# Two heads beside each other in PSUM: 64-column matmuls in the first batch's query phase

## The chip, the cores and the metric

The kernel runs on one core of a Trainium2 chip. The core has five engines that work side by side, each on its own list of instructions in a fixed order: PE (matrix multiply, whose weight loads the profile lists apart as PEld), DVE (elementwise work and reductions), ACT (activation functions and copies), POOL (elementwise work, SBUF only) and SP, which here starts most of the DMA transfers. SBUF is the working memory of 128 partitions. PSUM is the memory that PE writes its sums to; here it is used as tiles of 128 partitions by 512 floats. The metric is the time of one execution in microseconds (us).

## The reference, cut to what matters

```python
# q, k, v: (8 batches, 8 heads, 576 tokens, 64); w_phi: (64, 128)
def phi(x):
    proj = einsum('bhsd,df->bhsf', x, w_phi)
    proj = proj - max(abs(proj), axis=-1, keepdims=True)
    return concatenate([exp(proj), exp(-proj)], axis=-1)     # 256 features
q_p, k_p = phi(q), phi(k)
kv  = einsum('bhsf,bhsd->bhfd', k_p, v)
z   = sum(k_p, axis=2)
num = einsum('bhsf,bhfd->bhsd', q_p, kv)
den = einsum('bhsf,bhf->bhs', q_p, z)[..., None] + 1e-6
x   = (num / den), tokens by heads*64                        # 4608 x 512
h   = x @ w_in                                               # 512 -> 2048
out = maximum(0.01 * h, h) @ w_out                           # 2048 -> 512
```

It is linear attention with an exponential feature map, followed by a two-layer network over all 4608 tokens. All of it is float32.

## The kernel before, in words

Two heads make a pair: partitions 0 to 63 hold the first, 64 to 127 the second. A batch has four pairs. Attention of a pair has a key phase, which sums `kv` and `z` over the tokens, and a query phase, which gives `num` and `den` for each token and divides. The network runs over blocks of 256 tokens; its matmuls split float32 into a high and a low part (`xh`, `xl`, `w0h`, `w0l`, `gh`, `gl`) and are most of PE's work. A tile program schedules all instructions: the code gives priorities (`tc.cur_priority`), the scheduler weighs them with estimated times and so fixes each engine's order when the kernel is built. A change of a few instructions can therefore move others anywhere in the program.

The first batch is special. Its four key phases (`first_k_phase`) run at the very start. Its query phase (`first_q_phase`) runs by token units instead of pair by pair: unit 0 is tokens 0 to 255, unit 1 tokens 256 to 511 (four pairs each, one group of instructions per pair), unit 2 the last 64 tokens of all four pairs in one group. That makes nine groups. After unit 0 the first block of the network can begin, after unit 1 the second. Meanwhile `load_weights` (lines 187 to 197) prepares the network's weights, three ACT, DVE and POOL steps for each of 32 slices.

One group of the query phase goes like this. PE projects the tokens (L440). DVE takes the largest absolute value and subtracts it (L523, L525). PE transposes the result (L531) into PSUM. ACT computes both exponentials for both heads, `ee[0]` and `ee[1]` (L538, L539); the tiles are `eq` or `qs` in the profile. PE then multiplies by the pair's `kvs_of` (tiles `f`), whose 128 columns are the 64 columns of `kv` and 64 copies of `z`: for one head, partitions 0 to 63 of the PSUM tile `nm` receive the numerator and 64 to 127 the denominator (L553). The two heads `j` stand beside each other along the free dimension. ACT copies each head's numerator into the ring of attention outputs (L556, tile `ring`) and its denominator, with 1e-6 added, into `dn` (L557), each on 64 partitions. DVE transposes `dn`, takes the reciprocal of one value per token and transposes back (L560, L562, L563, tile `mb`), and POOL multiplies (`x`, L74). `nm` is tile `h` in unit 0 (two buffers) and tile `c` in units 1 and 2 (one buffer). The tile `dn` has two buffers.

A float32 matmul of this phase is one instruction in the program and two records in the profile, each with its own weight load. The network's split matmuls (L611 to L633, type fp32r) make one.

Of the kernel before, what the change touches and what calls it, by code (L numbers as in the profile page):

```python
# [13 lines left out]
AF = mybir.ActivationFunctionType  # L14
# [31 lines left out]
def attention_moe_kernel(ctx: ExitStack, tc: tile.TileContext, q, k, v, w_phi, w_in, w_out, out):  # L46
    nc = tc.nc
# [8 lines left out]
    def st(shape, dt, tag, name=None):  # L56
        return pools.get(tag, sp).tile(shape, dt, tag=tag, name=name or tag, bufs=BUFS.get(tag, 1))
# [18 lines left out]
    def pt(tag):  # L76
        return ps.tile([P, 512], F32, tag=tag, name=tag, bufs=PBUFS[tag])
# [140 lines left out]
    kvs_of = {}  # L218
# [290 lines left out]
    def first_q_phase(u):  # L509
        t0, w = units[u]  # L510
        rq = first_q[u]
        tail = u == 2
        if tail:
            rq = rq.rearrange("p a t -> p (a t)").unsqueeze(1)
            w = NP * w
        n, ns = P, 2
        for hp in range(1 if tail else NP):
# [14 lines left out]
            if hp % 2:  # L532
                ee = st([P, 2, S], F32, "qs")
                ee = [ee[:, t, 0 : 2 * w] for t in range(2)]
            else:
                ee = [st([P, 2, U], F32, "eq").rearrange("p a b -> p (a b)")[:, 0 : 2 * w] for t in range(2)]
            ee = [x.rearrange("p (j t) -> p j t", j=2) for x in ee]
            nc.scalar.activation(ee[0], tr, AF.Exp)  # L538
            nc.scalar.activation(ee[1], tr, AF.Exp, scale=-1.0)  # L539
            yield  # L540
            nm = pt("c" if u else "h")[:, 0 : 2 * w].rearrange("p (j t) -> p j t", j=2)
            dn = st([P, U], F32, "dn")[:, 0:w]
            x = ring[:, 0, :, t0:S] if tail else ring[:, 0, hp : hp + 1, t0 : t0 + w]
            m = x.shape[1]

            def heads(y):
                return y.rearrange("p (a t) -> p a t", a=m)

            for j in range(2):
                for h in range(m):  # L550
                    ts = slice(w // m * h, w // m * h + w // m)
                    for t in range(2):
                        nc.tensor.matmul(nm[:, j, ts], lhsT=kvs_of[hp + h][0][:, j, t], rhs=ee[t][:, j, ts],  # L553
                                         start=t == 0, stop=t == 1)
                rr = slice(64 * j, 64 * j + 64)
                nc.scalar.copy(x[rr], heads(nm[0:64, j]))  # L556
                nc.scalar.activation(dn[rr], nm[64:128, j], AF.Copy, bias=1e-6)  # L557
            yield
            dt = st([P, U], F32, "mb")[:, 0:w]
            nc.vector.transpose(dt, dn)  # L560
# [96 lines left out]
    together(first_k_phase(0), first_k_phase(1))  # L657
    together(first_k_phase(2), first_k_phase(3))
    together(first_q_phase(0))
    split(0)  # L660
    tc.cur_priority = PU
    first_load_q(1)
    first_load_q(2)
    together(first_q_phase(1))
    split(1, *xb)
    together(first_q_phase(2))
    for t in range(TT):
        accs[1, t] = pt(('h', 'a')[t])
# [59 lines left out]
```

## Time and profile before

| what | value |
|---|---|
| three runs, median (lowest to highest) | 1168.24 us (1168.23 to 1170.24) |
| the profiled execution's own time | 1168.86 us |
| its span in the profile | 1167.1 us |
| PE busy over the span | 1141.4 us (98%) |
| DVE, ACT, POOL busy | 737.9, 854.7, 652.0 us |
| the matmuls of L553 start between | 40.1 and 83.5 us |
| ACT in L556 and L557, 18 instructions each | 6.54 and 6.85 us |

The span is what the profiler saw from the first to the last instruction; the time of an execution has 1.8 us more around it. In rows of the profile a line such as `L553 PE MATMUL c<-eq,f 128*128 128x64 f32 x32` names the line of the kernel, the engine, the operation, the tile written and the tiles read, the part of the PE array used (rows*columns), the shape and the number of records. A row of waits names the waiting engine and line, what it waited for, the total in us, how often, and the longest. Rows of the chain give start, length and the work that held up the end.

### The profile page before, as it was taken

The numbers are of one execution on the slowest core, as the hardware profiler recorded it, in microseconds if no ns is written. First come the engines' busy times: TensorE is split into PE (matmuls) and PEld (weight loads), VectorE is DVE, ScalarE is ACT, GpSimd is POOL, SyncE is SP. The second block draws the span as 40 slices with busy tenths as digits, with TensorE's granted clock in tenths as the row PEclk, the third lists the DMA queues.
The fourth block names the chain that finished last, engine by engine and source line by source line (L and its number), as shares of the span: only waits on it lengthen the run. The fifth ranks groups of instructions, "written<-read, shape, count | busy, mean of one in ns | idle before, by whom it ended". The sixth has DMA issues, their size and how long they took to land.

```text
span 1167.1 us, 21441 instructions
## 1 busy us (share of the span) xinstructions
PE 1141.4 (98%) x7496; PEld 1024.0 (88%) x7496; DVE 737.9 (63%) x1316; ACT 854.7 (73%) x2256; POOL 652.0 (56%) x702
## 2 busy tenths in 40 slices
PE   8899999999999999999999999999999999999998
PEld 5677778899999999889999999999899999999997
DVE  6878996587767767767777767646777675100000
ACT  5777786888887888878888888868888885433232
POOL 1451222567666677676777666766566665433232
PEclk9999999999999999999999999999999999999999
DMA  8435432211111111101111111101111100000000
GB/s 222 139 90 153 123 102 53 60 43 33 52 34 51 34 41 34 51 23 34 49 25 52 33 52 34 52 12 41 34 51 34 41 2 12 10 20 10 10 19 19
DMA packets 69980, 57.87 MB, mean 50 GB/s; under 512 B 52208, under 2 KB 53488, under 8 KB 69872
## 3 DMA queue, kind: packets, MB, share of 16 engines
q1 hardware_dynamic: 67120, 55.78, 17.0%
q8 instruction: 59, 0.97, 0.3%
q10 hardware_dynamic: 2752, 0.72, 0.3%
q14 instruction: 49, 0.40, 0.1%
HBM read 46.27 MB, written 9.44 MB: 48 GB/s over the span
## 4 chain that ended last, share of the span: by engine, by line
PE 80%; DVE 8%; ACT 5%; DMA 3%; issue 2%; POOL 1%; SPq 1%; ACTq 0%; DVEq 0%; POOLq 0%
PE h L611 10%; PE h L612 10%; PE h L614 10%; PE acc L631 10%; PE acc L632 10%; PE acc L633 10%; PE c L242 7%; PE a L419 3%; PE a L424 2%; PE a L421 2%; PE a L265 2%; DVE tq L396 1%; PE a L379 1%; PE a L380 1%; PE h L476 1%
## 5 line engine op out<-in xcount | busy, mean ns | idle before, releaser
L74 POOL TENSOR_TENSOR gl<-g,gh 128x256 fp32r<-128x256 f32 x288 | 236.7, 825 | 311.7 <-ACT gh L69 226.9
L611 PE MATMUL h<-xh,w0h 128*128 128x256 f32 x1088 | 275.5, 282 | 3.3 <-ACT g L618 1.6
L612 PE MATMUL h<-xh,w0l 128*128 128x256 f32 x1088 | 272.7, 280 | 0.0
L611 PEld LDWEIGHTS h<-xh,w0h 128*128 128x128 f32 x1088 | 205.1, 189 | 14.0 <-ACT g L618 3.1
L631 PE MATMUL acc<-w1h,gh 128*128 128x512 f32 x544 | 214.3, 394 | 0.1
L632 PE MATMUL acc<-w1l,gh 128*128 128x512 f32 x544 | 213.4, 392 | 0.0
L612 PEld LDWEIGHTS h<-xh,w0l 128*128 128x128 f32 x1088 | 205.0, 188 | 7.7
L633 PE MATMUL acc<-w1h,gl 128*128 128x512 f32 x544 | 204.6, 394 | 0.3 <-POOL gl L74 0.3
L614 PE MATMUL h<-xl,w0h 128*128 128x256 f32 x1088 | 191.7, 281 | 0.0
L618 ACT ACTIVATE g<-h 128x256 f32<-128x256 f32 x288 | 108.5, 380 | 100.8 <-PE h L614 81.7
L74 POOL TENSOR_TENSOR ql<-eq,qh 128x576 fp32r<-128x576 f32 x96 | 145.4, 1527 | 45.2 <-DVE qh L410 39.9
L69 ACT CAST gh<-g 128x256 fp32r<-128x256 f32 x288 | 115.1, 402 | 62.3 <-PE acc L632 60.7
L614 PEld LDWEIGHTS h<-xl,w0h 128*128 128x128 f32 x1088 | 155.6, 189 | 0.8 <-issue 0.4
L74 POOL TENSOR_TENSOR kpl<-ek,kph 128x512 fp32r<-128x512 f32 x72 | 103.1, 1432 | 75.7 <-ACT kph L69 58.9
L71 DVE COPY o<-acc 128x512 f32<-128x512 f32 x17 | 11.7, 688 | 165.2 <-DMA out_dram<-o 125.1
L633 PEld LDWEIGHTS acc<-w1h,gl 128*128 128x128 f32 x544 | 100.1, 188 | 15.9 <-POOL gl L74 1.0
L631 PEld LDWEIGHTS acc<-w1h,gh 128*128 128x128 f32 x544 | 102.3, 188 | 12.2 <-ACT kvl L192 0.4
L632 PEld LDWEIGHTS acc<-w1l,gh 128*128 128x128 f32 x544 | 102.3, 188 | 11.3
L295 ACT ACTIVATE ek<-pmk,m4n 128x128 f32<-128x128 f32 (+1 forms) x240 | 90.1, 392 | 10.4 <-DVE m4n L279 7.7
L296 ACT ACTIVATE ek<-pmk,m 128x128 f32<-128x128 f32 (+1 forms) x240 | 89.4, 390 | 10.3 <-DVE m L273 8.5
L410 DVE TENSOR_REDUCE qh<-eq 128x576 fp32r<-128x576 f32 x96 | 69.6, 751 | 26.3 <-ACT eq L404 23.6
L270 DVE TENSOR_TENSOR pmk<-a,pmk 128x256 f32<-128x256 f32 (+1 forms) x120 | 49.2, 419 | 51.9 <-ACT pmk L69 50.3
(186 smaller groups left out, 2382.4 us busy)
## 6 DMA issues: line engine op xcount, KB each, us to landing
out_dram<-o SPq DMA_DIRECT2D x36, 256.0 KB, 2.0
rv<-in_v_dram SPq DMA_DIRECT2D x28, 320.0 KB, 3.6
rq<-in_q_dram SPq DMA_DIRECT2D x28, 288.0 KB, 2.9
rk<-in_k_dram SPq DMA_DIRECT2D x27, 288.0 KB, 2.9
ring<-in_w_in_dram SPq DMA_DIRECT2D x9, 512.0 KB, 3.6
f<-in_w_out_dram SPq DMA_DIRECT2D x7, 512.0 KB, 3.7
f<-in_w_in_dram SPq DMA_DIRECT2D x7, 512.0 KB, 3.7
ring<-in_w_out_dram SPq DMA_DIRECT2D x5, 512.0 KB, 6.0
```

The costliest lines, as they stand in the source:

```text
L69: nc.scalar.copy(o, i)
L74: (nc.vector if pick(key) == "v" else nc.gpsimd).tensor_tensor(o, a, b, op=op)
L242: nc.tensor.matmul(kvp[0 : lt.shape[1], 256 * j : 256 * j + 256], lhsT=lt, rhs=rt, start=first and j == 0, stop=last, skip_group_check=True)
L295: nc.scalar.activation(ek[r, j, 0:F], pmk[r, h], AF.Exp, bias=m4n[r, h : h + 1])
L296: nc.scalar.activation(ek[r, j, F:256], pmk[r, h], AF.Exp, scale=-1.0, bias=m4[r, h : h + 1])
L611: nc.tensor.matmul(ph, lhsT=weight(0, "h", ft)[:, d * P : d * P + P], rhs=xh[d], start=d == 0, stop=False)
L612: nc.tensor.matmul(ph, lhsT=weight(0, "l", ft)[:, d * P : d * P + P], rhs=xh[d], start=False, stop=False)
L614: nc.tensor.matmul(ph, lhsT=weight(0, "h", ft)[:, d * P : d * P + P], rhs=xl[d], start=False, stop=d == NP - 1)
L618: nc.scalar.activation(g, ph, AF.Prelu, alpha=0.01)
L631: nc.tensor.matmul(a, lhsT=gh[:, ts], rhs=weight(1, "h", ft), start=ft == 0, stop=False)
L632: nc.tensor.matmul(a, lhsT=gh[:, ts], rhs=weight(1, "l", ft), start=False, stop=False)
L633: nc.tensor.matmul(a, lhsT=gl[:, ts], rhs=weight(1, "h", ft), start=False, stop=ft == NFT - 1)
```

## The change

In `nm` the free dimension now separates numerators (`c` = 0) from denominators (`c` = 1), and the partitions separate the heads: head `j` goes to partitions 64j to 64j+63. So each matmul uses 64 of the 128 columns of `kvs_of`, and writes one half of the partitions. There are eight of them in a group where there were four (32 where there were 16 in the last group), in the order numerator then denominator, within them by exponential `t`, and innermost by head `j`, so that one head's half and the other's alternate. ACT reads each of the two halves of the free dimension in one instruction on 128 partitions, the denominators first.

```diff
-            nm = pt("c" if u else "h")[:, 0 : 2 * w].rearrange("p (j t) -> p j t", j=2)
+            nm = pt("c" if u else "h")[:, 0 : 2 * w].rearrange("p (c t) -> p c t", c=2)
...
-            for j in range(2):
+            for c in range(2):
                 for h in range(m):
                     ts = slice(w // m * h, w // m * h + w // m)
                     for t in range(2):
-                        nc.tensor.matmul(nm[:, j, ts], lhsT=kvs_of[hp + h][0][:, j, t], rhs=ee[t][:, j, ts],
-                                         start=t == 0, stop=t == 1)
-                rr = slice(64 * j, 64 * j + 64)
-                nc.scalar.copy(x[rr], heads(nm[0:64, j]))
-                nc.scalar.activation(dn[rr], nm[64:128, j], AF.Copy, bias=1e-6)
+                        for j in range(2):
+                            nc.tensor.matmul(nm[64 * j : 64 * j + 64, c, ts], lhsT=kvs_of[hp + h][0][:, j, t, 64 * c : 64 * c + 64],
+                                             rhs=ee[t][:, j, ts], start=t == 0, stop=t == 1)
+            nc.scalar.activation(dn, nm[:, 1], AF.Copy, bias=1e-6)
+            nc.scalar.copy(x, heads(nm[:, 0]))
```

In the changed kernel the matmul is on line 554, the denominators' read on line 556 and the numerators' on line 557. On PE, at the start of unit 0 (tile `h` is the groups' `nm`, `a` and `acc` the projections and transposes, `c` the last key phase's transposes):

```order
 L486 MATMUL c<-ident,kvs 128x66 x4
-L553 MATMUL h<-eq,f_107 128x256 x2
+L554 MATMUL h<-eq,f_107 64x256 x8
 L531 MATMUL a<-ident,pm 128x128 x4
 L440 MATMUL acc<-bd,ks 128x256 x2
 L486 MATMUL c<-ident,kvs 128x66 x4
-L553 MATMUL h<-eq,f_107 128x256 x2
 L531 MATMUL a<-ident,pm 128x128 x4
-L553 MATMUL h<-qs,f_106 128x256 x2
-L553 MATMUL h<-eq,f_109 128x256
+L554 MATMUL h<-qs,f_106 64x256 x8
+L554 MATMUL h<-eq,f_109 64x256 x8
```

A group's two heads stood in two places, with other work between them; now its eight matmuls stand in one place, where the first two were. On ACT at the same place:

```order
 L187 ACTIVATE ql<-ring 128x512
-L556 COPY ring<-h 64x256
-L557 ACTIVATE dn<-h 64x256
+L556 ACTIVATE dn<-h 128x256
+L557 COPY ring<-h 128x256
 L538 ACTIVATE qs<-a 128x512
 L539 ACTIVATE qs<-a 128x512
+L192 ACTIVATE kvl<-ring 128x512
 L488 COPY f_108<-c 128x4x64
 L489 COPY f_108<-c 128x4x64
-L192 ACTIVATE kvl<-ring 128x512
-L556 COPY ring<-h 64x256
```

The pair of reads of the first head has become the pair of reads of both, and the second head's pair, which stood behind L192, is gone. On DVE, the seven instructions around the first group's transposes (`ql` are the weights in preparation), before:

```order
L523 TENSOR_REDUCE m_427<-acc 128x4
L190 SCALAR_TENSOR_TENSOR ql<-ring,ql 128x512
L525 TENSOR_TENSOR pm<-acc,m_427 128x512
L560 STREAM_TRANSPOSE mb<-dn 128x256
L193 ISA ql<-ql,kvl 128x1024
L562 RECIPROCAL rc<-mb 128x8
L563 STREAM_TRANSPOSE mb<-rc 128x256
```

and in the changed kernel:

```order
L560 STREAM_TRANSPOSE mb<-dn 128x256
L190 SCALAR_TENSOR_TENSOR ql<-ring,ql 128x512
L523 TENSOR_REDUCE m_433<-acc 128x4
L562 RECIPROCAL rc<-mb 128x8
L193 ISA ql<-ql,kvl 128x1024
L525 TENSOR_TENSOR pm<-acc,m_433 128x512
L563 STREAM_TRANSPOSE mb<-rc 128x256
```

The same seven instructions stand in another order: the transpose of the denominators has moved ahead of the weight step L190 and of the next group's L523.

## The prediction

> **What bounds the kernel now.** I read the busy shares first, then the stretch in which the changed lines run, then who waits for whom there, and last the single instructions.
>
> ```profile
> PE 1141.4 (98%) x7496; PEld 1024.0 (88%) x7496; DVE 737.9 (63%) x1316; ACT 854.7 (73%) x2256; POOL 652.0 (56%) x702
> ```
>
> Over the whole span the matmul engine PE is the bound: it is idle for 1167.1 - 1141.4 = 25.7 us. Work taken from ACT can only pay by shortening those idle times; work added to PE costs its full length wherever PE has none. The changed lines run from 40 to 85 us. The table by stretch (each engine's busy time) says how tight each engine is there:
>
> ```profile
> core 0: us, PE busy (x) PEld busy (x) DVE busy (x) ACT busy (x) POOL busy (x), PEclk, DMA share, GB/s
> 40.00:70.00 30.00, 24.53 (x127) 18.60 (x126) 28.09 (x55) 25.52 (x60) 17.64 (x19) 1.00 0.36 107
> 110.00:1130.00 1020.00, 1011.68 (x6808) 921.49 (x6807) 654.13 (x1159) 769.06 (x2060) 604.22 (x633) 1.00 0.14 40
> ...
> 70.00:85.00 15.00, 14.87 (x90) 13.05 (x89) 9.87 (x23) 9.19 (x26) 7.68 (x10) 1.00 0.27 70
> ```
>
> In 40 to 70 us DVE is the tightest engine: 28.09 of 30 us, since it also prepares the weights there (L188 to L193). PE is idle for 30 - 24.53 = 5.5 us. From 70 to 85 us PE is idle for 0.13 us only: there it is the bound again. From 110 to 1130 us it is idle for 8.3 of 1020 us. The granted clock is 1.00 throughout. The waits of 40 to 70 us (total, times, longest), PE's first, then DVE's:
>
> ```profile
> PE c L553 <- ACT dn L557: 1.4, 2, 1.0
> PE c L486 <- ACT kvs L69: 1.2, 1, 1.2
> PE h L553 <- ACT eq L538: 1.2, 1, 1.2
> PE h L611 <- ACT xh L69: 1.2, 2, 0.9
> PE a L531 <- DVE pm L525: 0.9, 2, 0.5
> PE c L553 <- ACT eq L538: 0.4, 1, 0.4
> ...
> DVE m L523 <- PE a L440: 1.1, 1, 1.1
> DVE ql L188 <- ACT ql L187: 0.4, 1, 0.4
> DVE mb L560 <- ACT dn L557: 0.2, 1, 0.2
> ```
>
> PE mostly waits for ACT here (L486's wait lies before 40 us; the others on ACT are 1.4 + 1.2 + 1.2 + 0.4 = 4.2 us). DVE waits only 1.1 + 0.4 + 0.2 = 1.7 us, and that is the most by which DVE's stretch can become shorter, whatever ACT saves.
>
> **The change part by part.** *ACT.* Before, each of the nine groups (four for the first 256 tokens, four for the second, one for the tail) copies a numerator and a denominator for each head, on 64 partitions; after, one of each on 128.
>
> ```profile
> L557 ACT ACTIVATE dn<-c 64x256 f32<-64x256 f32 x10 | 3.8, 380 | 1.3 <-DVE mb L560 1.1
> L556 ACT COPY ring<-c 64x256 f32<-64x256 f32 x10 | 3.6, 364 | 6.2 <-PE c L553 6.1
> L618 ACT ACTIVATE g<-h 128x256 f32<-128x256 f32 x288 | 108.5, 380 | 100.8 <-PE h L614 81.7
> ```
>
> The 128x256 read of PSUM by L618 takes 380 ns, the 64x256 ones 380 and 364: the other 64 partitions are free. So 18 instructions go, 9 x (0.364 + 0.380) = 6.7 us of ACT. In 42 to 54.5 us the chain runs along ACT with six such pairs; three go, 2.2 us, more than DVE's 1.7 us of waiting:
>
> ```profile
> 44.49 0.59 issue
> 45.08 0.36 ACT ring L556
> 45.47 0.39 ACT dn L557
> 45.88 0.45 DVE mb L560
> ...
> 53.91 0.58 ACT ql L187
> 54.51 1.33 DVE ql L188
> 55.87 0.44 DVE ql L189
> 56.33 0.69 DVE ql L190
> ```
>
> From 54.5 us the chain is DVE's own work, so what ACT saves later is slack. Against it: ACT now starts after the whole group, where before it read the first head while PE computed the second. And the denominator is read first, so DVE's transpose L560 has it one copy (0.36 us) sooner after the group's end. What is late next is DVE. Bounds of this term: 0 (the order or the longer group eats it) and -1.7 us (all of DVE's waiting goes); I take -1.2, since all three waits stand behind ACT in this stretch, L523's through PE's 1.2 us wait for L538.
>
> *PE.* Before, a group is 4 matmuls of 128 columns by 256 tokens; after, it is 8 of 64 columns. In the trace a full fp32 matmul makes two records:
>
> ```profile
> 71.16 0.86 PE c L553 x4
> ...
> 85.06 3.45 PE c L242 x16
> ```
>
> Four records (two matmuls) take 0.86 us, 0.216 each; L242's 16 records, with 66 columns only, take 0.216 each as well. So a matmul of half the columns costs a whole one unless two of them run side by side. A group was 8 records, 1.73 us; it is now 16. End one, no overlap: +1.73 us for each of eight groups, +13.8 us. End two: two matmuls on different column halves run side by side. The two records of one matmul use the same half and must follow each other, so a pair can share only the second record of one and the first of the next: 16 records in 9 steps, +0.216 a group, +1.7 us. No row of this trace shows two matmuls on two halves. The nearest rows are the weight loads, which run under the matmuls: PEld is busy for 18.60 us of the 24.53 in which PE is. I choose overlap, at two to one: the halves have their own columns, weights, moving data and PSUM partitions, and the two alternate in the order.
>
> The Trainium skill, "TensorE: Matmul & The Clock Gate", section "Part 3: Packing small matmuls — row/col tiling", says that matmuls on different column tiles run at once, with a start a few ns apart, and reports 2.38 times for three column tiles. No run here shows it; by it this term would be the small end.
>
> Where does +1.7 go? Six of the eight groups lie in 40 to 70 us, where PE's 5.5 us of idle time take them; the two after 70 us cost 2 x 0.216 = +0.4 us. Without the cover it is +1.7 in all.
>
> *The tail group* (64 tokens, four pairs): 32 records of 128 columns become 64 of 64 columns.
>
> ```profile
> 78.44 2.00 PE c L553 x16
> ...
> 82.08 1.73 PE c L553 x16
> ...
> L242 PEld LDWEIGHTS c<-kst,vhl x96: 133/136/138, 238.7 to 972.0; 128*64 128x64 f32 x48, 128*66 128x66 f32 x48
> ...
> L553 PEld LDWEIGHTS c<-eq,f x48: 186/192/192, 53.5 to 83.5; 128*128 128x128 f32 x48
> ```
>
> 3.73 us for 32, so down to 0.108 each with 64 tokens, half of the 0.216 for a quarter of the tokens: the weight load sets it. A load of 64 columns records 136 ns against 192, 56 less for 64 fewer columns, so half a load is about 0.054 us: 64 x 0.054 = 3.5 us. Ends: -0.2 and, were each still 0.108, +3.2. I take 0, at the row with 64 columns.
>
> *The order.* The scheduler moves instructions in the whole program. DVE's order around the groups holds the same weight work. PE's 8.3 us of waits after 110 us may come out an us more or less; I add nothing to the sum and 1 us to each side.
>
> **Sum:** -1.2 + 0.4 + 0 = -0.8 us. The profiled execution took 1168.86 us (span 1167.1 and 1.8 around it), 0.6 above the median: 1168.86 - 0.8 = 1168.1 there, 1167.4 as a median.
>
> **The rivals.** *No overlap (slower).* PE runs the halves one after the other: +13.8 us, decided by the step between records staying at 0.216. Idle time of 40 to 70 us hides part of it, at most 5.5: +8.3 to +13.8, in the middle +11, 1179.3 us. For it: no row shows an overlap. Against it: nothing that the two halves share is seen in the rows.
>
> *ACT's relief goes through (faster).* PE's 4.2 us of waits for ACT in 40 to 70 us vanish, less 0.4 to 1.7 for PE's added steps: about -3.2, 1165.0 us. For it: ACT loses a fifth of its work there (half of 13 pairs, 4.8 of 25.52 us). Against it: DVE has 28.09 us of work to do in the same 30, and PE's inputs come from DVE.
>
> *The weight loads bind.* If the 16 loads of a group, 0.136 each, ran end to end: 2.2 us, +0.45 a group, +3.6; in the tail 64 x 0.136 = 8.7, +5.0; less some 3 us of idle time, +5.6, 1173.8 us. Against it: 192 ns loads come every 108 ns in the tail.
>
> *A drain at each change of the array's division.* Each group goes from full to half columns and back, 18 times in all. A lone record lasts 0.379 us and a streamed one takes 0.216, so a drain is some 0.16 us: +2.9 on A's sum, 1170.3 us. The row that speaks is L242 later on, where loads of 64 and 66 columns alternate:
>
> ```profile
> 653.59 0.28 PE L612 MATMUL h<-xh,w0l 128*128 128x256 f32 x1
> 653.71 0.28 PE L611 MATMUL h<-xh,w0h 128*128 128x256 f32 x1
> 653.83 0.64 PE L242 MATMUL c<-kph,vhl 128*66 128x256 f32 x4
> 654.30 0.28 PE L612 MATMUL h<-xh,w0l 128*128 128x256 f32 x1
> ...
> L242 PE MATMUL c<-kph,vhl 128*64 128x256 f32 x192 | 50.1, 281 | 0.0
> ```
>
> Four records from 653.83 to 654.30 are 0.117 each, as L611's 0.12 without a change, and PE stood idle for 0.0 before the 64-column form: no drain. The Trainium skill, "TensorEngine Tiling (Array Packing)", section "Key Properties", says that changing the tiling mode drains the engine. This trace does not agree, so far as 64 and 66 columns are two modes; by the rule, this rival's sum would hold.
>
> **How the numbers follow.** A, overlap with DVE as the bound: 0.50, 1167.4, own range 1165.5 (-1.7 and 1 for the order) to 1170.0 (+1.7 unhidden). No overlap 0.22, relief through 0.17, loads bind 0.06, drain 0.05. A measurement tells some 0.2% (2.3 us) from no change. Faster: most of relief through, 0.15, and A's lower edge, 0.07: 0.22. Slower: no overlap, loads, half of the drain, and A's upper edge: 0.22 + 0.06 + 0.03 + 0.04 = 0.35. Within: 0.43. The range reaches down past relief through (1164.5) and up to the middle of no overlap (1179.5); some 0.2 is outside.
>
> **What would show it.** In the changed profile L554's 16 records of a group (one matmul is two) should take about 1.9 us from first to last, near 0.12 a record; 3.5 us means no overlap, and the time is then near 1179. The two ACT groups should show nine instructions each, 128x256, near 380 ns; 440 or more would make the ACT saving smaller. DVE should stay above 93% from 40 us to the last group. PE's idle time before 110 us should be some 1 to 3 us less. The prediction is wrong if the records of one group take over 2.2 us, if PE's idle time after 110 us moves by more than 2 us from 8.3 (then the order decided, not the change), or if the waits for ACT in the stretch vanish and PE's busy time fills them.

## The result, and the profile after

| | before | after |
|---|---|---|
| median of 6 runs each on one chip (lowest to highest) | 1169.01 us (1166.37 to 1170.35) | 1180.64 us (1177.91 to 1185.43) |
| ratio, 95% interval | | 1.0106 [1.0092, 1.0120] |
| profiled execution, its span | 1168.86, 1167.1 us | 1178.88, 1177.1 us |

The changed kernel is 11.6 us slower. The forecast was 1167.4 us in a range up to 1179.5. The busy times of the page after, for the whole span:

```profile
PE 1144.6 (97%) x7592; PEld 1019.5 (87%) x7592; DVE 752.4 (64%) x1316; ACT 845.6 (72%) x2238; POOL 659.4 (56%) x702
```

PE is busy 3.2 us more (1144.6 against 1141.4) in a span that is 10.0 us longer, so most of the loss is PE standing idle. I read the changed groups first, then the stretches.

The timeline of PE after, at a full group of 256 tokens, and at the tail group (start, length from the first record's start to the last one's end, line and operation, records):

```profile
59.67 1.03 PE L440 MATMUL a<-bd,f 128*128 128x256 f32 x4
60.63 1.95 PE L554 MATMUL c<-qs,f 128*64 128x256 f32 x16
62.51 0.38 PE L611 MATMUL h<-xh,w0h 128*128 128x256 f32 x1
62.73 0.28 PE L612 MATMUL h<-xh,w0l 128*128 128x256 f32 x1
...
76.08 0.82 PE L633 MATMUL acc<-w1h,gl 128*128 128x512 f32 x2
76.84 2.08 PE L554 MATMUL c<-eq,f 128*64 128x64 f32 x64
78.85 1.35 PE L440 MATMUL a<-bd,rk 128*128 128x256 f32 x5
```

and of PE before, where a head's matmuls of 128 columns follow the same projections, and where others stand ahead of the network's L611 and L612:

```profile
64.51 1.03 PE L440 MATMUL a<-bd,rq 128*128 128x256 f32 x4
65.38 1.03 PE L553 MATMUL c<-qs,f 128*128 128x256 f32 x4
...
76.55 1.03 PE L553 MATMUL c<-qs,f 128*128 128x256 f32 x4
77.23 0.47 PE L611 MATMUL h<-qh,w0h 128*128 128x256 f32 x1
77.53 0.28 PE L612 MATMUL h<-qh,w0l 128*128 128x256 f32 x1
```

The halves run side by side. Sixteen records take 1.95 us; their starts in the trace come in eight pairs, 6 to 7 ns within a pair and 0.216 us from pair to pair. The group's price is at its edges. Before, L553 starts 0.87 us after four records of L440, which is 4 x 0.216. After, L554 starts 0.96 us behind them: 0.09 more. The second pair comes 0.267 us behind the first: 0.05 more. From the last record's start to L611 it is 0.31 us where a step is 0.216: another 0.09. And L612 starts 0.22 us behind L611, where 0.118 is usual: 0.10 more. From L440's start to L612's it is 62.73 - 59.67 = 3.06 us, where 12 steps of 0.216 and one of 0.118 are 2.71: 0.35 more. Before, the same sum comes out even: 77.53 - 76.55 = 0.98 us, and 4 x 0.216 + 0.118 = 0.98. The blocks that no wait interrupts cost 0.30 us (ahead of the transposes L531) to 0.38 us. The eight groups stand in seven blocks, since two follow each other directly, so their edges cost some +2.3 us. The tail's 64 records of 64 tokens run in pairs 0.058 us apart, 1.9 us for 32 pairs and 0.36 for the edges, where 32 records took 0.112 each, 3.6 us, before: some -1.4 us.

ACT's reads in the groups of the page, denominators L556 and numerators L557 (busy us, mean ns, idle before):

```profile
L556 ACT ACTIVATE dn<-c 128x256 f32<-128x256 f32 x5 | 1.9, 373 | 3.9 <-DVE mb L560 2.9 <-PE c L554 1.0
L557 ACT COPY ring<-c 128x256 f32<-128x256 f32 x5 | 1.8, 362 | 0.0
L556 ACT ACTIVATE dn<-h 128x256 f32<-128x256 f32 x4 | 1.5, 384 | 0.7 <-PE h L554 0.7
L557 ACT COPY ring<-h 128x256 f32<-128x256 f32 x4 | 1.5, 379 | 0.0
```

They are 18 reads of 362 to 384 ns in place of 36. The busy times by stretch, after:

```profile
40.00:70.00 30.00, 23.85 (x176) 15.50 (x176) 28.73 (x51) 18.81 (x45) 18.25 (x19) 1.00 0.31 89
70.00:85.00 15.00, 14.61 (x136) 11.22 (x137) 11.08 (x28) 9.79 (x27) 8.46 (x12) 1.00 0.46 137
110.00:1130.00 1020.00, 1005.02 (x6730) 911.82 (x6729) 662.76 (x1152) 762.46 (x2050) 605.92 (x628) 1.00 0.14 39
200.00:400.00 200.00, 192.86 (x1302) 174.23 (x1301) 147.80 (x255) 161.15 (x442) 131.77 (x134) 1.00 0.16 43
400.00:600.00 200.00, 195.27 (x1328) 177.40 (x1327) 146.99 (x250) 159.24 (x436) 134.71 (x131) 1.00 0.14 37
```

and the last two of them before:

```profile
200.00:400.00 200.00, 198.30 (x1360) 181.72 (x1359) 142.62 (x257) 168.23 (x460) 130.59 (x137) 1.00 0.16 43
400.00:600.00 200.00, 197.73 (x1364) 181.58 (x1363) 150.06 (x264) 167.65 (x456) 136.69 (x134) 1.00 0.15 41
```

ACT has 6.7 us less to do in 40 to 70 us (18.81 against 25.52), DVE as much as it had (28.73, 28.09). The clock is 1.00 in all these stretches. The loss is far from the edit. From 200 to 600 us PE starts 2630 records (1302 + 1328) where it started 2724 (1360 + 1364): 94 fewer, and at 400 us for 2724 records (0.147 each) that is 13.8 us of work not done. PE's idle time from 110 to 1130 us is 1020 - 1005.02 = 15.0 us; it was 8.3.

PE's waits after, first in 40 to 70 us, then the longest in 200 to 600 us (total, times, longest):

```profile
PE a L531 <- DVE pm L525: 4.8, 3, 2.4
PE c L486 <- ACT kvs L69: 0.9, 1, 0.9
PE h L554 <- ACT qs L538: 0.2, 1, 0.2
```

```profile
PE c L242 <- POOL kpl L74: 1.9, 2, 0.9
PE a L419 <- DVE pmk L270: 1.7, 1, 1.7
PE a L419 <- DVE qh L410: 1.3, 3, 0.6
PE a L379 <- DVE tq L381: 1.1, 2, 0.6
PE a L265 <- DVE ks L228: 1.0, 1, 1.0
PE c L242 <- ACT gh L69: 0.8, 1, 0.8
PE h L611 <- ACT g L618: 0.8, 1, 0.8
```

and before, in 200 to 600 us, its longest ones:

```profile
PE a L419 <- DVE qh L410: 0.8, 1, 0.8
PE c L242 <- POOL kpl L74: 0.7, 1, 0.7
PE c L242 <- DVE kpl L74: 0.4, 1, 0.4
```

Near the edit, the waits for ACT have gone and DVE's have come in their place. In 200 to 600 us the seven rows shown make 8.6 us of waits, nearly all of them matmuls of the attention of later batches (L242 to L419) that wait for DVE, POOL or ACT. None of these instructions was edited; what changed for them is the order.

### The profile page after: what moved, and what is told of

The parts are those of the page before. It is cut to its first block, busy times and chain, and to the rows that moved or that the text cites. A ratio compares the mean times of both kernels' runs of the same rounds, so it can differ in the third digit from the quotient of the medians.

```text
span 1177.1 us, 21654 instructions
## 1 busy us (share of the span) xinstructions
PE 1144.6 (97%) x7592; PEld 1019.5 (87%) x7592; DVE 752.4 (64%) x1316; ACT 845.6 (72%) x2238; POOL 659.4 (56%) x702
## 4 chain that ended last, share of the span: by engine, by line
PE 68%; DVE 12%; ACT 10%; issue 4%; DMA 3%; POOL 2%; SPq 0%; ACTq 0%; DVEq 0%; POOLq 0%
PE h L614 9%; PE h L611 9%; PE h L612 9%; PE acc L631 8%; PE acc L632 8%; PE acc L633 8%; PE c L242 5%; PE a L419 2%; PE a L424 2%; DVE tq L396 2%; PE a L421 2%; DVE ks L228 2%; PE a L265 2%; DVE ql L190 1%; POOL ql L74 1%
## 5 line engine op out<-in xcount | busy, mean ns | idle before, releaser
L74 POOL TENSOR_TENSOR gl<-g,gh 128x256 fp32r<-128x256 f32 x288 | 233.8, 816 | 323.8 <-ACT gh L69 253.3
L611 PE MATMUL h<-xh,w0h 128*128 128x256 f32 x1088 | 277.3, 284 | 0.5 <-ACT g L618 0.5
L612 PE MATMUL h<-xh,w0l 128*128 128x256 f32 x1088 | 273.7, 280 | 0.0
L631 PE MATMUL acc<-w1h,gh 128*128 128x512 f32 x544 | 213.9, 393 | 0.8 <-ACT gh L69 0.8
L611 PEld LDWEIGHTS h<-xh,w0h 128*128 128x128 f32 x1088 | 205.1, 189 | 10.2 <-issue 1.9
L612 PEld LDWEIGHTS h<-xh,w0l 128*128 128x128 f32 x1088 | 205.0, 188 | 7.9
L633 PE MATMUL acc<-w1h,gl 128*128 128x512 f32 x544 | 200.1, 394 | 0.8 <-POOL vhl L118 0.6
L614 PE MATMUL h<-xl,w0h 128*128 128x256 f32 x1088 | 188.4, 281 | 0.1
L74 POOL TENSOR_TENSOR ql<-eq,qh 128x576 fp32r<-128x576 f32 x96 | 148.2, 1559 | 36.5 <-DVE qh L410 34.2
L74 POOL TENSOR_TENSOR kpl<-ek,kph 128x512 fp32r<-128x512 f32 x72 | 106.1, 1474 | 63.7 <-ACT kph L69 53.5
L631 PEld LDWEIGHTS acc<-w1h,gh 128*128 128x128 f32 x544 | 102.2, 188 | 13.6 <-ACT gh L69 1.2
L632 PEld LDWEIGHTS acc<-w1l,gh 128*128 128x128 f32 x544 | 102.2, 188 | 11.5
```

Source lines behind the costliest of these rows:

```text
L74: (nc.vector if pick(key) == "v" else nc.gpsimd).tensor_tensor(o, a, b, op=op)
L611: nc.tensor.matmul(ph, lhsT=weight(0, "h", ft)[:, d * P : d * P + P], rhs=xh[d], start=d == 0, stop=False)
L612: nc.tensor.matmul(ph, lhsT=weight(0, "l", ft)[:, d * P : d * P + P], rhs=xh[d], start=False, stop=False)
L614: nc.tensor.matmul(ph, lhsT=weight(0, "h", ft)[:, d * P : d * P + P], rhs=xl[d], start=False, stop=d == NP - 1)
L631: nc.tensor.matmul(a, lhsT=gh[:, ts], rhs=weight(1, "h", ft), start=ft == 0, stop=False)
L632: nc.tensor.matmul(a, lhsT=gh[:, ts], rhs=weight(1, "l", ft), start=False, stop=False)
```

## The experiments

Theory ORDER: the order that the scheduler gave the changed kernel costs the time, whatever the edit does. Rival EDIT: the new matmuls and reads, or what they set off later, cost it. To part them I fixed the order by hand: each engine's instructions are chained in a written order, by dependencies that add no semaphore. The groups' matmuls and reads moved into a function at the end of the file, so that the other line numbers stay; in these kernels the 64-column matmul is L747, the 128-column one L763, its denominator read L767.

```diff
-            nm = pt("c" if u else "h")[:, 0 : 2 * w].rearrange("p (c t) -> p c t", c=2)
...
+            dn, x, heads = numerators(nc, pt, st, ring, groups, kvs_of, ee, u, tail, w, hp, t0)
...
+    keep_order(tc, groups)
...
+        for a, b in zip(line, line[1:]):
+            tc.add_manual_dep(b, a.name, info, reason="order")
```

For many of these kernels I give how much time PE lost in a stretch. It is worked out so: each record of PE outside the groups is given the median time, in the kernel before, from the start of a record of its line and shape to the next start; the stretch's length less the sum of these for the records started in it is lost. One profiled execution each:

```text
us lost by PE in               110-200  200-400  400-600  600-end
before                           13.6      5.4      5.1      2.2
edit, old order (1st, 2nd run)   13.0 13.0  6.5 6.1  6.0 4.3  2.0 1.3
groups alone, old order          13.5      8.6      5.6      1.9
tail alone, old order (1st, 2nd) 13.5 12.1  5.3 5.3  5.1 5.2 -0.3 0.5
reads behind both heads          13.6      6.3      4.2      1.3
heads in turn, old order         14.7      6.2      4.0      1.4
after                            14.0     13.7      9.7      1.0
after, numerators read first     12.5     14.4      9.7      1.0
old edit, new order              15.1     15.9      8.6      2.0
old edit, new order from 150 us  15.2     14.8      8.0      1.3
edit, new order from 150 us      14.8     13.4      8.8      1.3
edit, new order up to 150 us     19.3      6.5      4.0     -0.1
edit, new order from 400 us      13.1      6.0      9.3      2.5
after, PE's rows moved           14.0     17.9     14.5      1.1
```

**The edit in the old order.** Every instruction of the four lists that the edit doesn't touch stands where it stood before; a group's eight matmuls stand where the first head's stood, its reads behind them.

```diff
+    keep_order(tc, groups)
```

> The changed matmuls and reads, but every other instruction of each engine in the order of the kernel before (a group's matmuls stand where the first head's stood, its reads where the first head's reads stood). Theory ORDER (the edit itself gains 2 to 4 us in the first 85 us, the new order after 200 us loses about 12): 1164 to 1168 us, the groups' 16 records in 1.8 us each, PE idle 8 us between 110 and 1130 us. Rival EDIT (the matmuls on halves or the joint reads delay the later work): 1177 to 1183 us, as the changed kernel.

Measured: 1167.57 us (1164.17 to 1169.78) against 1169.22, ratio 0.9987 [0.9975, 0.9999]. A second measurement, on another chip:

> The whole edit in the order of the kernel before, once more, on one chip with its parts. PARTS ADD UP: groups alone plus tail alone, within 1 us. If the groups cost nothing, it is as fast as the tail alone; if they cost 2 to 3 us, it is that much slower than the tail alone.

Measured: 1167.87 us against 1168.62, the same ratio, 0.9987 [0.9977, 0.9997]. So the edit by itself makes the kernel 0.8 to 1.6 us faster, less than the 2 to 4 us that ORDER gave it. EDIT falls.

**The new order with the old edit.** The complement, the four matmuls and four reads of the kernel before, with the lists of the changed kernel (`NEW` names the groups that have the edit):

```diff
-NEW = set(range(9))
+NEW = set(())
```

> The old matmuls of 128 columns and the four reads of 64 partitions a group, with every other instruction in the order of the changed kernel. ORDER: 1180 to 1185 us, the changed kernel's time plus the 2 to 4 us that the edit gains. EDIT: 1167 to 1171 us, as the kernel before.

Measured: 1193.00 us (1191.07 to 1196.20), ratio 1.0207 [1.0189, 1.0225]. The direction is ORDER's, the size is not: 24 us, twice the loss to explain. A later run showed why: here both heads' matmuls stand next to each other, which costs some 10 us of its own (below). So this run parts nothing cleanly, and I made it again with the groups where they had stood.

**The old kernel, new order from 150 us.** All instructions are those of the kernel before; up to 150 us all lists are its own too, groups included, and from there the changed kernel's.

```diff
-NEW = set(range(9))
+NEW = set(())
...
+            if n <= -100:
+                g, k = divmod(-100 - n, 40)
+                line.append(groups[g][0 if e == "PE" else 1][k])
```

(The three added lines let each instruction of a group have a place of its own in the list.)

> The kernel before, its instructions unchanged, in its own order up to 150 us on every engine (each head's matmuls and reads of the groups where they stood), and from there in the changed kernel's order. ORDER ALONE: the changed kernel's order after 150 us costs some 12 us whatever the query phase does; the run with the edit and this seam was 1182.05 us, the edit gains 1.6: 1180 to 1185 us, with PE busy 4 to 8 us less from 200 to 600 us than before. RIVAL, ORDER AND EDIT TOGETHER (the loss needs the edit's other times of the query phase): below 1173 us.

Measured: 1181.67 us (1178.86 to 1181.96) against 1169.04, ratio 1.0099 [1.0083, 1.0115], which is 9.7 to 13.4 us. Its stretches of 200 to 600 us:

```profile
200.00:400.00 200.00, 192.88 (x1293) 173.38 (x1292) 144.72 (x246) 161.20 (x442) 129.30 (x133) 1.00 0.15 42
400.00:600.00 200.00, 196.35 (x1341) 178.94 (x1340) 147.85 (x252) 160.81 (x441) 136.25 (x133) 1.00 0.14 37
```

They hold 1293 + 1341 = 2634 records, nearly the changed kernel's 2630, without any of the edit. By the table the seam at 150 us costs 1.6 us (15.2 against 13.6 in 110 to 200 us), and 200 to 600 us lose 12.3 us more than before. The order alone makes the loss.

**Where in the order.** Three kernels with the edit and a seam in the lists: the new order up to 150 us and the old one behind it; the other way round; and the new order from 400 us only. Their only difference from each other is the list; the edit of the code is that of the first experiment.

> The edit, with the changed kernel's order for all instructions that started before 150 us in its profile, and the order of the kernel before for all others. ORDER: 1164 to 1168 us, since the changed kernel was 3 us ahead in work done at 150 us and the loss lies behind that. EDIT: 1177 to 1183 us.

> The edit, with the order of the kernel before for all instructions that started before 150 us in its profile, and the changed kernel's order for all others. ORDER: 1177 to 1183 us. EDIT: also 1177 to 1183 us. A third reading, that the order of the first 150 us is what counts (it sets what is late later): 1164 to 1168 us here and 1177 to 1183 us with the two orders the other way round.

> The edit, in the old kernel's order up to 400 us on every engine and in the changed kernel's order from there. ORDER OF EACH STRETCH: the changed order loses by its own rows wherever it stands; of its 12 us some 7 came by 400 us and 4 after, and the seam costs up to 3: 1171 to 1176 us, with PE's stalls in 400 to 600 us and not ahead of it. RIVAL, AN EARLY SLIP: the loss is carried in from rows between 150 and 400 us, 1167 to 1170 us. SECOND RIVAL, the whole loss lies after 400 us: 1179 to 1183 us.

Measured: new order up to 150 us 1170.75 us, 1.0016 [1.0007, 1.0024]; from 150 us 1182.05 us, 1.0117 [1.0099, 1.0134]; from 400 us 1174.32 us, 1.0038 [1.0024, 1.0052]. The first lies 2.8 us above the range of ORDER, the two others lie in theirs. The table of lost time agrees with all three: a stretch in the old order loses 5.3 to 8.6 us (200 to 400) and 4.0 to 6.0 (400 to 600), one in the new order 13.4 to 15.9 and 8.0 to 9.7, whatever stands before it. In the first of the three the seam at 150 us costs some 5 us itself (19.3 in 110 to 200 us), which accounts for the miss. So no slip is carried in from an early place: each stretch of the new order loses by its own rows.

**Whose rows.** In the changed kernel, the places where PE waited in 225 to 575 us often have network matmuls right behind the waiting attention matmul. I put such matmuls ahead of it, at 11 places, on PE only. One of them (`a` and `c` are the attention's tiles):

```diff
+L631 MATMUL acc<-w1h_112,gh 128x512
+L632 MATMUL acc<-w1l_113,gh 128x512
+L631 MATMUL acc<-w1h_112,gh 128x512
+L632 MATMUL acc<-w1l_113,gh 128x512
+L611 MATMUL h<-xh,w0h_119 128x256
+L612 MATMUL h<-xh,w0l_120 128x256
+L611 MATMUL h<-xh,w0h_119 128x256
 L242 MATMUL c<-kph,vhl 66x256
 L242 MATMUL c<-kph,vhl 64x256
 L242 MATMUL c<-kph,vhl 66x256
 L242 MATMUL c<-kph,vhl 64x256
 L242 MATMUL c<-kpl,vhl 66x256 x2
-L631 MATMUL acc<-w1h_112,gh 128x512
-L632 MATMUL acc<-w1l_113,gh 128x512
-L631 MATMUL acc<-w1h_112,gh 128x512
-L632 MATMUL acc<-w1l_113,gh 128x512
-L611 MATMUL h<-xh,w0h_119 128x256
-L612 MATMUL h<-xh,w0l_120 128x256
-L611 MATMUL h<-xh,w0h_119 128x256
```

> The changed kernel in its own order on ACT, DVE, POOL and SP; on PE alone 11 rows of matmuls of the network are put ahead of 11 attention matmuls at which PE waited in 225 to 575 us (over nominal 1.94, 1.18, 0.98, 0.75, 0.68, 1.09, 0.75, 0.74, 0.47, 0.72 and 1.09 us, 10.4 in all). Same work. PE'S ROWS: the loss is work that stood behind a waiting matmul and could have run; it comes back by half or more: 1180.6 - 5 to 10 = 1170 to 1176 us, with stretches 200 to 600 us holding some 35 to 65 records of matmuls more than the 2630 of the changed kernel (0.146 us each). RIVAL, THE OTHER ENGINES' ORDER: DVE, POOL and ACT deliver late and the waits come back a few matmuls further on: 1178 to 1183 us.

Measured: 1187.48 us (1184.43 to 1189.40), ratio 1.0153 [1.0130, 1.0175], some 5 us slower still than the changed kernel's 1.0106 and above both ranges. PE's waits of 200 to 600 us in it:

```profile
PE h L611 <- ACT xh L69: 6.5, 3, 3.9
PE acc L631 <- ACT gh L69: 4.0, 3, 2.3
PE a L419 <- DVE qh L410: 1.9, 4, 1.1
PE h L611 <- ACT g L618: 1.1, 2, 0.8
```

The matmuls that I moved forward weren't ready either: L611 and L631 now wait for ACT, up to 3.9 us, since ACT's list makes their inputs (`xh`, `gh`) behind the attention's. In the profiled execution up to 3.4 us are clock: behind the waits of 3.9 and 2.3 us the granted clock is 0.50 in 230.1 to 233.5 and in 581.7 to 585.1 us. Even without them the time lies far above the 1170 to 1176 us of PE'S ROWS, so that theory falls. A wait of PE at an attention matmul is where the loss shows; the lists of PE, ACT, DVE and POOL seem to make it together, but no run here has one engine's new list beside the others' old ones, so that is not shown.

**Small changes of the writing order.** Two kernels leave the work as it is and change which of the two reads is written first, so that the scheduler orders anew.

```diff
-                nc.scalar.copy(x[rr], heads(nm[0:64, j]))
                 nc.scalar.activation(dn[rr], nm[64:128, j], AF.Copy, bias=1e-6)
+                nc.scalar.copy(x[rr], heads(nm[0:64, j]))
```

> The kernel before, with the two reads of each head written in the other order, the denominator ahead of the numerator: the same instructions and the same work; the scheduler then gives PE an order with some 320 rows of difference in 5900. ANY ORDER BUT THE OLD ONE IS WORSE (the kernel before stands in a fortunate order, a re-sort costs some us wherever it comes from): 1174 to 1185 us, with the loss in PE's stalls of 200 to 600 us. RIVAL, THIS NEW ORDER ALONE IS POOR (orders differ by an us or so, as my prediction had it, and the changed kernel's one is an unlucky one): 1167.5 to 1171.5 us.

> The changed kernel, with the two reads of a group written in the other order, the numerator ahead of the denominator: the same work, and an order from the scheduler that differs from the changed kernel's by 47 rows on PE, all near the query phase; after 200 us it is the changed kernel's. ORDER AFTER 200 US: it keeps the changed kernel's loss, 1178 to 1183 us. RIVAL, THE FIRST 110 US SET IT (the loss later is a consequence of when buffers and transfers of the first stages come free): a few rows near the groups change it, below 1175 us.

Measured: the kernel before with denominators first 1170.32 us against 1167.86, 1.0020 [1.0011, 1.0029]; the changed kernel with numerators first 1179.98 us, 1.0094 [1.0081, 1.0107]. The second keeps the changed kernel's loss (14.4 and 9.7 in the table), so these rows of the first 110 us don't set it. The first is inside the range of the rival, but it doesn't decide what I wanted: in the trace its records on PE stand in another order only from 67 to 180 us, and behind that the order is the old one. It shows that a reorder of the early rows alone moves 2 us, nothing of how other orders of 200 to 600 us would do.

**What the parts of the edit are worth, in the old order.** First the tail alone, with the eight other groups in the old form:

```diff
-NEW = set(range(9))
+NEW = set((8,))
```

> The edit in the tail group alone (64 matmuls of 64 columns by 64 tokens, two reads instead of four), the eight groups of 256 tokens as before, every other instruction in the order of the kernel before. TAIL GAINS: its 64 records take about 2.0 us, where the 32 before took 3.73; PE is idle for 0.13 us only in 70 to 85 us, so the 1.7 us come off the end: 1169.2 - 1.7 = 1167.5 us, and then the eight other groups give nothing in the run that has the whole edit in the old order (1167.57). RIVAL, THE GROUPS OF 256 TOKENS GAIN (ACT's relief, my prediction's -1.2) and the tail gives nothing: 64 records in about 3.7 us and 1169.2 us.

Measured: 1176.48 us (1174.95 to 1181.05) against 1167.86, 1.0076 [1.0061, 1.0090], which neither theory allowed. Its PE timeline at two groups, then its waits of 40 to 85 us:

```profile
47.88 1.13 PE L763 MATMUL h<-qs,f 128*128 128x256 f32 x4 [1.81 <-ACT dn L767]
48.84 1.03 PE L763 MATMUL h<-eq,f 128*128 128x256 f32 x4
51.87 1.13 PE L763 MATMUL h<-eq,f 128*128 128x256 f32 x4 [2.00 <-ACT dn L767]
```

```profile
PE h L763 <- ACT dn L767: 6.1, 4, 2.0
PE c L763 <- ACT dn L767: 5.4, 3, 3.3
```

In this kernel each group's second head stands right behind its first, and its four records wait up to 3.3 us until ACT has read the first head's denominators out of the same PSUM tile: 11.5 us in all. In the kernel before, other work stood between the heads and covered most of that (1.4 us of such waits are left there). The run with the old edit in the new order had the same fault, 14.7 us of such waits. To see whether that is the cause, I kept the old matmuls next to each other, in all nine groups, and wrote the four reads behind both heads:

```diff
             for j in range(2):
                 for h in range(m):
...
+        for j in range(2):
             rr = slice(64 * j, 64 * j + 64)
             act.append(nc.scalar.copy(x[rr], heads(nm[0:64, j])).ins)
```

> The old edit (128 columns, a head at a time, four reads of 64 partitions), the matmuls of both heads next to each other and the four reads behind both of them; all other instructions in the order of the kernel before. THE WAIT BETWEEN THE HEADS IS THE READS' (one PSUM tile: the second head's matmuls wait until ACT has read the first head's part): the 11.5 us of PE's waits for ACT's denominator reads between the heads vanish, PE is idle for some 6 us in 40 to 85 us, and the time is within 2 us of before, 1166 to 1170 us. RIVAL, THE HALVES' SAVING ON ACT IS WHAT COUNTS (18 reads fewer): ACT's four reads a group then hold DVE up by 0.7 us a group, 1172 to 1176 us.

Measured: 1170.32 us (1169.36 to 1172.17) against 1169.04, 1.0013 [1.0004, 1.0022], 0.3 us above the first theory's range and below the rival's 1172. PE's waits for L767 are gone from 40 to 85 us, and so is the time. So the edit's merged reads, which stand behind both heads, remove a wait that the old kernel paid for only in part.

Then the tail alone again, with the eight groups exactly where they stood, and the eight groups alone:

```diff
-NEW = set(range(9))
+NEW = set((8,))
...
-NEW = set(range(9))
+NEW = set(range(8))
```

> The edit in the tail group alone, and the eight groups of 256 tokens exactly as before: each head's matmuls and reads in the places where they stood. (In the run before this one of the same edit the two heads' matmuls stood next to each other, and PE waited 11.5 us between them for ACT's reads of the first head.) TAIL GAINS: its 64 records take some 2.0 us in place of 3.73; PE has no idle time there, so 1.7 us off the end, 1166.2 to 1167.5 us. RIVAL, THE EIGHT GROUPS GAIN, the tail's time is lost again later: 1167.9 to 1169.2 us, as before.

> The edit in the tail group alone, once more, on one chip with the other parts. TAIL GAINS its 1.7 us and no more: 1.2 to 2.2 us below the kernel before. RIVAL, the 4.5 us of the first look are its own: 4 to 5 us below.

> The edit in the eight groups of 256 tokens, the tail group as before, every other instruction in the order of the kernel before. The whole edit in that order was 1.6 us below the kernel before, the tail alone 4.5 us below it, on another chip. GROUPS COST: the difference is the groups' own (both heads' matmuls in one block ahead of the reads, PE's waits for DVE's L525 up from 0.9 to 4.6 us): 2 to 3 us above the kernel before. RIVAL, GROUPS NEITHER GAIN NOR COST (what lies between the two is PE's single waits of 0.7 to 0.9 us after 600 us, which come and go): within 1 us of the kernel before.

Measured: the tail alone 1164.58 us, 0.9960 [0.9947, 0.9973], and on the next chip 1165.43 us, 0.9977 [0.9964, 0.9990]; the groups alone 1170.81 us, 1.0017 [1.0005, 1.0030]. The tail alone beats both kernels; it gains 3.2 to 4.5 us, between and above what my theories allowed, and the groups lose 2.2. On the one chip the parts add up: -3.2 + 2.2 = -1.0, the whole edit -0.8. What I can't fully explain is their sizes. At 110 us all of them are 1.1 to 1.8 us of work ahead of the kernel before, by the table's measure. The rest comes later, in lists that are the same to the last row: the groups alone lose 3.2 us more than before in 200 to 400 us, the tail alone 1.7 to 2.5 less behind 600 us. A start that is an us earlier or later seems to meet other waits in the same list. A part of the whole edit's time is the clock (last section).

**Do the halves need to alternate?** All matmuls of one head's half ahead of the other's, in the old order:

```diff
-        for c in range(2):
-            for h in range(m):
-                for t in range(2):
-                    for j in range(2):
+        for j in range(2):
+            for c in range(2):
+                for h in range(m):
+                    for t in range(2):
```

> The edit, with every other instruction in the order of the kernel before, and in each group all matmuls of one column half ahead of all of the other: the same matmuls, the halves no longer alternate. SHARED BY ALTERNATION (the two halves run together because neighbours in the order use different halves): the 16 records of a group go back to one each 0.216 us, 3.5 us from first to last instead of 1.77, 8 x 1.7 = +13.8 us of PE; the stretch from 40 to 85 us of the run with the edit in the old order has 5.9 us of idle PE (30 - 24.21 and 15 - 14.89) to hide some of it; the tail's 64 records, 2.0 us there, go to between 3.5 (the prediction's half loads) and 6.9 (0.108 each). Sum 1167.6 + 8 to 18 = 1175.5 to 1186 us. RIVAL, QUEUES OF THEIR OWN (each half takes its matmuls as they come, whatever stands between): records still in pairs, 1.8 us a group, 1166 to 1170 us.

Measured: 1173.07 us (1172.31 to 1173.30) against 1167.86, 1.0041 [1.0028, 1.0053]. Its PE timeline at a full group and at the tail:

```profile
65.10 2.86 PE L747 MATMUL c<-qs,f 128*64 128x256 f32 x16
...
83.24 3.77 PE L747 MATMUL c<-eq,f 128*64 128x64 f32 x64
```

A group takes 2.86 us instead of 1.95, the tail 3.77 instead of 2.08: 8 x 0.91 + 1.69 = 9.0 us more work for PE. The kernel is some 6 us slower than the edit in the old order (1.0041 - 0.9987 = 0.0054 of 1168); idle time hides the rest. Alternation is what makes the pairs, as the first theory had it, but the time is below its range, since a group costs less than its 3.5 us. The starts in the trace tell why: the first four records of the group stand alone, then come four pairs with starts 6 to 57 ns apart, then four alone.

## Why the prediction was wrong, point by point

- *Overlap of the halves.* Right, and more complete than predicted: 16 records in eight steps, not nine. I had let the two records of one matmul follow each other on their half; the trace pairs every record with one of the other half. The run with the heads in turn shows the size at stake, 9.0 us of PE, with pairs partly left.
- *The price of a group.* I had +0.216 us from the ninth step. There is none, but the edges of a block cost 0.30 to 0.38, some +2.3 us for eight groups in seven blocks; that my +1.7 without cover was near this is luck. The cause is that of the rival with a drain at each change of division, and its 0.16 us a change, two changes a block, was the right size. I had ruled it out by L242's rows with 64 and 66 columns. Other rows of L242, in the same trace, show it (last section).
- *The tail.* I took 0 from half weight loads at 0.054 us each. Pairs of loads run side by side too, 0.058 us a pair, so the term is -1.4, below my lower end of -0.2. In the run with the heads in turn, where few records pair, it takes 3.77 us, about the 3.73 of before: all of the gain is pairing.
- *ACT's relief, and DVE late next.* Right as a mechanism: waits for ACT in 40 to 70 us fall to 0.9 + 0.2 us, those for DVE's L525 rise from 0.9 to 4.8, and DVE is busy for 28.73 of 30 us. But I said that before the change ACT read the first head while PE computed the second. It did not: the second head's matmuls wait for that read (11.5 us where nothing stands between).
- *The sum of the edit.* -0.8 us predicted; in the old order the edit measured -0.8 and -1.6. That the sum holds is luck, since its parts don't: the groups, -1.2 + 0.4 in my sum, measured +2.2 us alone, and the tail, 0 in my sum, -3.2 and -4.5. Only at 110 us are the groups alone where I had them, 1.1 us of work ahead of before; they lose it later.
- *The order: the step that failed.* "PE's 8.3 us of waits after 110 us may come out an us more or less; I add nothing to the sum and 1 us to each side." In the changed kernel they came out 6.7 us more in idle time, and 12 us more in lost time (38.4 against 26.3 in the table's sums). The old kernel with the new order from 150 us measured +9.7 to +13.4 us for it. I had treated the order as noise around the edit; it was the largest term, though a scheduler that orders the whole program was known. I compared the two orders only around the edit, not in 200 to 600 us. What I had named as the sign of this failure, PE's idle time after 110 us moving by over 2 us from 8.3, is what happened.
- *The rivals.* No overlap (1179.3 us) and binding loads (1173.8) rest on causes that the trace excludes. That 1179.3 lies close to the measured time is chance: its sign, a step of 0.216 between single records, isn't there. ACT's relief going through fails at DVE's 4.8 us. The drain is there, but its 1170.3 us knew nothing of the tail's gain and of the order.

What stays open: which pair of lists makes the new order lose in 200 to 600 us. It is not PE's alone at the places of its waits; no run mixes the lists of the engines; and nothing here says that the old order is good rather than the new one poor, beyond these two.

## What to carry to other kernels

Where a scheduler orders a whole program, cost an edit in two terms: the edit in the old order, and the reorder. The second can be ten times the first and lie hundreds of us away, so compare the lists there too, or pin the old order and measure the edit alone. Two matmuls on 64 columns each run as one when they alternate in the order; a block of them cost 0.30 to 0.38 us at its edges here, and two groups in one block paid that once. And when two parts of one PSUM tile are written and read in turn, look for the write that waits for the other part's read.

## What the runs showed of the hardware that I had not expected

- **Pairs of float32 records.** Half-array records start 6 to 7 ns apart and each pair takes the step of one: 0.216 us with 256 tokens, 0.058 with 64, weight loads included. The Trainium skill, "TensorE: Matmul & The Clock Gate", section "Part 3: Packing small matmuls — row/col tiling", says that column tiles overlap with starts a few ns apart; the trace agrees, at nearly twice the rate for two tiles.
- **Starts out of the program's order.** With the heads in turn, the first record of the second half (it is 430 ns long, as each half's first is; the others 379) starts 6 ns behind the fifth of the first half, ahead of three records that stand before it in the order. The Trainium skill, in the same section, says that matmuls start and end in program order; as I read these records, this run doesn't agree. That four records are the reach is an inference from one place in each group.
- **A change of division costs 0.30 to 0.38 us, in and out.** The step into a block of half columns is 0.09 us longer than usual, the next one 0.05, the step out 0.09, and the one behind it 0.06 to 0.11. At the edge no weight load runs under the matmul ahead of it: L554's first load starts 2 ns before its matmul, where L553's loads start 0.21 us before theirs. The kernel before has the same price where L242 uses 64 rows of the array:

```profile
102.51 0.28 PE L612 MATMUL h<-xh,w0l 128*128 128x256 f32 x1
102.72 1.08 PE L242 MATMUL c<-ek,rv 64*66 64x256 f32 x4
103.72 0.74 PE L614 MATMUL h<-xl,w0h 128*128 128x256 f32 x4
104.30 0.39 PE L631 MATMUL h<-w1h,gh 128*128 128x512 f32 x1
```

  From 102.51 to 104.30 it is 1.79 us, where four steps of 0.216 and five of 0.118 are 1.45: 0.34 more. The Trainium skill, "TensorEngine Tiling (Array Packing)", section "Key Properties", says that a change of tiling mode drains the engine; these edges agree. The 64 and 66 columns of L242 show nothing of it; why they don't is open.
- **The clock halves for 3.4 us behind waits that are shorter than that.** Busy time and granted clock of 50 to 60 us, with the heads in turn, and of 40 to 70 us, with the new order from 400 us and with the whole edit in the old order, whose lists are the same up to 400 us:

```profile
50.00:60.00 10.00, 7.63 (x40) 5.00 (x40) 8.36 (x16) 3.69 (x9) 3.89 (x5) 0.83 0.23 72
```

```profile
40.00:70.00 30.00, 24.70 (x163) 16.09 (x159) 24.05 (x46) 18.68 (x42) 15.42 (x17) 0.90 0.29 82
```

```profile
40.00:70.00 30.00, 24.21 (x180) 16.26 (x176) 27.72 (x52) 19.35 (x46) 17.96 (x19) 1.00 0.33 96
```

  PE's longest wait there is 2.4 us in all three, for DVE's L525. In the first the granted clock is 0.50 from 52.9 to 56.3 us, right behind that wait; in the second it is 0.50 in 52.9 to 56.3 us too, and in 39.3 to 42.7, behind a wait of 1.0 us; in the third it never dips. Half a clock for 3.4 us is 1.7 us of work lost. The Trainium skill, "TensorE: Matmul & The Clock Gate", section "Part 1: The HAM clock gate (the "warmup" mystery)", says that the clock halves after an idle window of about 3.4 us, and that these windows run on their own, so that each run meets them elsewhere; the length agrees, but the waits here are shorter than such a window. Of 24 executions of the whole edit in the old order, 14 had a mean clock of 0.998 or less; their times are 2 to 3 us above those of the six at 1.000. Of 82 of the kernel before, whose longest wait in 40 to 70 us is 1.2 us, it was 8. That the groups in one block, by their longer wait, bring the dips is what this points to; no run here took that wait away alone. In the changed kernel it was four of the six executions, at 0.994 to 0.998. Its profiled one has no dip and is 10.0 us longer than the profiled one before, so by my estimate one to two of the 11.6 us are clock.
